# A fused sparse-attention and feed-forward kernel: operands of its matmuls moved to 2 KB multiples, four softmax buffers, and small VectorE work moved to GpSimd and ScalarE

## The chip, the core and the metric

The kernel runs on one core of a Trainium2 chip. The metric is the device time of one execution in microseconds (us), lower is better. Before the change it is 938.36 us, the median of three runs (938.2 to 938.99).

## What is computed

Attention with 8 batches, 8 heads, 576 positions and head size 64, followed by a feed-forward network on the 4608 tokens. Heads 0 to 3 see the 32 newest positions ("local"), heads 4 to 7 see every 32nd position ("strided").

```python
scores = scale * np.matmul(q, k.transpose(0, 1, 3, 2))
mask_local = (rel >= 0) & (rel < stride)
mask_strided = (rel >= 0) & (pos[None, :] % stride == pos[:, None] % stride)
...
attn = np.exp(scores - max); attn = attn / (np.sum(attn, axis=-1, keepdims=True) + 1e-09)
x = np.matmul(attn, v)          # to (4608, 512), all heads side by side
h = x @ w_in                    # (4608, 2048)
g = 0.5 * h * (1.0 + erf(h * inv_sqrt2))
return g @ w_out                # (4608, 512)
```

## The kernel before

The 4608 tokens are nine tiles of 512 tokens (t = 0 to 8), and the hidden size 2048 is 16 slices (f = 0 to 15). A matrix is used as the sum of a rounded part and a small rest ("h" and "l" in the tile names: xlh and xll for the local heads, xsh and xsl for the strided ones, gh and gl for the activations; both parts of a weight slice lie in one slot w_wt), and each product is made of three matmuls.

**The dense steps.** For each t and f, line 672 forms the hidden slice in a PSUM bank: 12 matmuls with a 128x128 stationary block of w_wt and 512 columns of x moving. ScalarE applies Gelu (line 697) and rounds (line 698, gh), VectorE takes the rest (line 700, gl), and line 709 multiplies with the second weight matrix: 12 matmuls with gh or gl stationary and 512 columns of w_wt moving. TensorE's order is written out at the end of the kernel (lines 788 to 798): hidden slice n, then output product n-1. So the Gelu of a slice has one output product and one hidden product of time. In tile 0 the first four slices run in two halves of 256 tokens (HALVES = 4), which makes 96 hidden matmuls of 256 columns; the other 3408 large matmuls move 512 columns.

**Weights.** weights(f) loads a packed slice of 1 MB into a slot and unpacks it: two ScalarE passes (lines 290, 291), a VectorE merge (line 293), a rounding (line 302) and a rest (line 307, VectorE or GpSimd). Slots have one tag "w" with 17 buffers of 8 KB per partition, and the attention of the first rows (tiles 0 and 1) borrows them.

**Local attention of the next tile**, local(t). At step f = 2 TensorE makes the scores of tile t+1 (line 366), at f = 13 the products with v (line 407). Between them, for four groups j: a masked maximum on VectorE (line 426, four instructions, writes a pt tile), four exponentials on ScalarE (line 433), for each pair of groups an addition of 1e-9 and a reciprocal (lines 438, 439), the quotient (line 443, VectorE or GpSimd), a 32x32 transpose (line 447), and eight small DMAs from pt to bt, issued by SyncE (line 396). The pt tiles have two buffers (line 413), so group 2 needs the buffer of group 0 and group 3 that of group 1.

**Strided attention of the next tile**, unit(): GpSimd multiplies (lines 556, 573), VectorE sums (lines 561, 578), and finish() makes the softmax: maximum and subtraction (lines 502, 503), exponential on ScalarE (line 511), sum, addition of 1e-9, reciprocal and product on VectorE (lines 506 to 509). turn() transposes the result (line 518) and split() rounds it on ScalarE (line 324) and takes the rest on VectorE (line 329). opening() does the same for tiles 0 and 1, all batches at once.

**The order.** Every operation is handed to a planner (Plan.add) with the engines that may run it, its cost there, and a due time. Plan.run plays this forward and writes the instructions of each engine in the order that it found; the chip then runs each engine's list in that order. Its costs come from lines 253 to 266 (STEP = 5.43 us for a dense step, T0 = 17 us for the start).

**Output.** Each tile's four PSUM banks are copied to ob tiles (line 716, two buffers) and stored by SyncE (line 728).

In the program's allocation before, the large operands do not start at multiples of 2 KB within a partition: the w slots start 1824 bytes past one, xl 1120, xs 1632, gh and gl 1632.

Of the kernel before, what the change touches and what calls it, by code (L numbers as in the profile page):

```python
# [16 lines left out]
U16 = mybir.dt.uint16  # L17
AF = mybir.ActivationFunctionType
# [3 lines left out]
P = 128  # L22
# [6 lines left out]
UR = 4  # L29
FIRST, VISIT = 2, 13  # L30
HALVES = 4
# [32 lines left out]

class Part:
# [7 lines left out]
class Op:  # L73
    def __init__(self, eng, fn, deps, due, bufs, table, kb, name, rel):
        self.eng, self.fn, self.deps, self.due, self.bufs = eng, fn, deps, due, bufs
        self.table, self.kb, self.name, self.rel = table, kb, name, rel
        self.start = self.end = None


class Plan:  # L80
# [9 lines left out]
    def add(self, eng, fn, deps=(), due=0.0, bufs=(), table=None, kb=0, name="", rel=None):  # L90
        op = Op(eng, fn, [d for d in deps if d is not None], due,
                [b.buf if isinstance(b, Part) else b for b in bufs], table, kb, name,
                due - self.ahead if rel is None else rel)
        for b in op.bufs:
            b.left += 1
        self.ops.append(op)
        return op

    def run(self, busy):
# [8 lines left out]
        nxt, now, state, dma = 0, 0.0, "e", 0.0  # L108
        events = []
# [15 lines left out]
        pe_done = set()  # L125
        h_end = 0.0
        while count < len(self.ops):
            moved = False
            for e in free:
# [3 lines left out]
                for op in waiting[e]:  # L133
# [10 lines left out]
                    if any(room[k] < v for k, v in need.items()):  # L144
                        continue
                    if e == "ACT" and op.table == "e" and state == "g":
                        ready = sum(x.eng[e] for x in waiting[e] if x.table == "e" and at[x] <= now)
                        if (ready < 1.2 and now < at[op] + 5.0) or now - 0.1 < h_end < now + 2.0:
                            continue
# [16 lines left out]
                op.end = now + dur  # L166
                if e == "PE":
# [3 lines left out]
                if op.kb:  # L171
                    dma = max(dma, now + 0.9) + op.kb / 400.0
# [35 lines left out]
def attn_ffn_kernel(ctx: ExitStack, tc: tile.TileContext, qk, vl, vl0, q0, k0, v0, q1, k1, v1, qs, ks, vs, w, out):  # L208
    nc = tc.nc
    NT = qk.shape[0]  # L210
# [26 lines left out]
    def slot(name, dtype=F32):  # L237
        return buf("w", [P, 4 * DM], name, NF + 1, dtype)
# [24 lines left out]
    T0 = 17.0  # L263
    LOSS = 3.4

    def at_step(n):
        return T0 + 2.0 + n * STEP + (n // NF) * LOSS

    def at_pass(n):
        return T0 + n * 2.9 if n < 2 * HALVES else at_step(n - HALVES)  # L270
# [4 lines left out]
    def weights(f):  # L275
        raw, wt = slot(f"raw{f}"), slot(f"wt{f}")
        lead = buf("lead", [P, 2 * DM], f"{f}", 2, F16)
        due = at_pass(f) - 3.0 if f <= HALVES else at_step(f) - 3.0
        views = {}

        def load(e):
# [7 lines left out]
        o0 = plan.add({"SP": 0.5}, load, [lo_of.get(f - 3)], due - 12 if f else 2.3, [raw], kb=1024, name=f"load{f}")  # L289
# [5 lines left out]
            [o2], due - 4, [raw], name=f"or{f}")  # L295
# [8 lines left out]
        o4 = plan.add({"DVE": 0.72, "ACT": 1.16}, hi, [o3], due - 3, [raw, wt], name=f"hi{f}")  # L304
# [4 lines left out]
        o5 = plan.add({"POOL": 2.4} if f > HALVES else {"DVE": 1.25, "POOL": 2.4} if f else {"DVE": 1.25}, lo, [o4], due - 2, [raw, wt], name=f"lo{f}")  # L309
# [4 lines left out]
    def x_bufs(t):  # L314
        local = [buf(f"xl{i}", [P, N2, TT], f"{t}", 1, F32R) for i in "hl"]
        strided = [buf(f"xs{i}", [P, DH, TT], f"{t}", 2, F32R) for i in "hl"]
# [5 lines left out]
    def split(src, dst, bufs, src_bufs, deps, due, n, name, psum_src=True):  # L322
# [7 lines left out]
        o2 = plan.add({"DVE": dve(n)}, low, [o1] + deps, due + 0.3, bufs + src_bufs, name=f"{name}l")  # L330
# [6 lines left out]
    def local(t):  # L337
# [3 lines left out]
        for a, b in ((0, 2), (2, 4)) if t == 0 else ((0, 4),):  # L341
            ld += [plan.add({"SP": 0.5}, lambda e, a=a, b=b: nc.sync.dma_start(
                lq()[:, a * JW:b * JW], qk[t][:, a * JW:b * JW]), [v_ops.get((t - 1, NJ - 1))],
                T + FIRST * STEP - 12 if t else 0.1 + a, [lq], kb=128 * 4 * (b - a) * JW / 1024, name=f"qk{t}")] * (b - a)
# [534 lines left out]
```

## Time and profile before

| | before |
|---|---|
| median of 3 runs | 938.36 us |
| the profiled execution, its own time | 939.23 us |
| its span | 937.5 us |
| mean granted TensorE clock | 0.975 |
| TensorE matmul busy | 870.9 us (93%) |
| VectorE busy | 529.7 us (57%) |
| ScalarE busy | 398.3 us (42%) |
| GpSimd busy | 463.5 us (49%) |

The span is taken inside the execution; 1.7 us of its time lie around it. PE is TensorE's matmuls, PEld its weight loads, DVE VectorE, ACT ScalarE, POOL GpSimd, SP SyncE, and SPq the queue in which SyncE issues DMAs. A busy TensorE is not TensorE at its peak, since matmuls overlap: what counts is the distance from start to start. Idle time of the other engines costs nothing unless TensorE waits for it.

### The profile page before, as it was taken

The page shows a single profiled execution, that of the slowest core. Times are in us where ns is not written, and L with a number is a line of the kernel's source. Part 1 is how long each engine was busy: PE and PEld are TensorE (multiplying, and loading weights), DVE is VectorE, ACT ScalarE, POOL GpSimd, SP SyncE. Part 2 cuts the span into 40 slices and gives each one's busy share as a digit, 9 for nine tenths or more (in the row PEclk, how much of TensorE's full clock was granted, in tenths as well). Part 3 has the DMA queues.
Part 4 walks back from the last instruction along what each step waited for, and adds up shares of the span by engine and source line. Part 5 has one row for each costly group of instructions (what it writes and reads, how often), then busy time and mean ns, then how long its engine had stood idle before and what let it go on. Part 6 is the DMA issues. An engine that isn't in the chain of part 4 may idle for free. (4 is left out here: it accounts for less than half of the span.)

```text
span 937.5 us, 15581 instructions
## 1 busy us (share of the span) xinstructions
PE 870.9 (93%) x6032; PEld 700.3 (75%) x6032; DVE 529.7 (57%) x1110; ACT 398.3 (42%) x808; POOL 463.5 (49%) x325
## 2 busy tenths in 40 slices
PE   2598799989999999899989999899999998999997
PEld 2486587768887888688867878687878886888885
DVE  4879757674667486435856664646676486111111
ACT  4769724643344345433552244433543344122111
POOL 4647576556566576445737754654576483000000
PEclk9999989989999999899998999999999999999999
DMA  9934222210231032002301211012210220001001
GB/s 373 391 135 182 80 69 46 101 34 4 79 117 46 1 124 95 19 3 102 116 12 53 83 49 58 11 58 105 66 58 26 80 73 17 3 1 45 1 1 45
DMA packets 27098, 69.43 MB, mean 74 GB/s; under 512 B 5904, under 2 KB 14096, under 8 KB 24720
## 3 DMA queue, kind: packets, MB, share of 16 engines
q1 hardware_dynamic: 27024, 68.44, 20.8%
q8 instruction: 47, 0.77, 0.3%
q14 instruction: 27, 0.22, 0.1%
HBM read 54.78 MB, written 9.44 MB: 69 GB/s over the span
## 5 line engine op out<-in xcount | busy, mean ns | idle before, releaser
L709 PE MATMUL banks<-w_wt,gh 128*128 128x512 f32 x1152 | 372.4, 405 | 11.3 <-ACT gh L698 11.2
L709 PEld LDWEIGHTS banks<-w_wt,gh 128*128 128x128 f32 x1152 | 220.9, 193 | 66.7 <-ACT gh L698 14.6
L709 PE MATMUL banks<-w_wt,gl 128*128 128x512 f32 x576 | 235.3, 408 | 23.3 <-DVE gl L700 23.3
L697 ACT ACTIVATE banks<-banks 128x512 f32<-128x512 f32 (+1 forms) x148 | 84.6, 571 | 377.2 <-PE banks L672 376.7
L700 DVE TENSOR_TENSOR gl<-banks,gh 128x512 fp32r<-128x512 f32 (+1 forms) x148 | 99.0, 670 | 202.2 <-ACT gh L698 202.0
L672 PE MATMUL banks<-xsh,w_wt 128*128 128x512 f32 (+1 forms) x592 | 165.3, 398 | 7.6 <-DVE w_wt L302 4.5
L672 PE MATMUL banks<-xlh,w_wt 128*128 128x512 f32 (+1 forms) x592 | 159.5, 388 | 0.0
L709 PEld LDWEIGHTS banks<-w_wt,gl 128*128 128x128 f32 x576 | 111.8, 194 | 56.1 <-DVE gl L700 29.5
L672 PEld LDWEIGHTS banks<-xsh,w_wt 128*128 128x128 f32 x592 | 112.3, 194 | 34.1 <-DVE w_wt L302 5.0
L672 PEld LDWEIGHTS banks<-xlh,w_wt 128*128 128x128 f32 x592 | 111.6, 190 | 23.7
L672 PE MATMUL banks<-xsl,w_wt 128*128 128x512 f32 (+1 forms) x296 | 92.4, 391 | 0.2 <-DVE xsl L329 0.2
L672 PE MATMUL banks<-xll,w_wt 128*128 128x512 f32 (+1 forms) x296 | 91.8, 389 | 0.0
L698 ACT CAST gh<-banks 128x512 fp32r<-128x512 f32 (+1 forms) x148 | 85.1, 575 | 4.6
L672 PEld LDWEIGHTS banks<-xsl,w_wt 128*128 128x128 f32 x296 | 56.6, 192 | 13.6 <-DVE xsl L329 0.5
L672 PEld LDWEIGHTS banks<-xll,w_wt 128*128 128x128 f32 x296 | 56.1, 190 | 11.6
L426 DVE CUSTOM_DVE_ANT_0 pt<-banks,mask 128x64 f32<-128x64 f32 x128 | 20.7, 221 | 57.4 <-DMA bt<-pt 53.6
L433 ACT ACTIVATE pt<-pt,lsm 128x64 f32<-128x64 f32 x128 | 42.9, 336 | 21.4 <-DVE lsm L426 16.6
L307 POOL TENSOR_TENSOR w_wt<-w_raw,w_wt 128x1024 fp32r<-128x1024 f32 x13 | 32.7, 2521 | 37.1 <-ACT w_wt L302 21.4
L697 ACT ACT_TABLE_LOAD x39 | 50.0, 1283 | 0.7
L293 DVE SCALAR_TENSOR_TENSOR w_raw<-w_raw 128x1024 uint32<-128x1024 uint32 x16 | 26.6, 1669 | 4.4 <-ACT w_raw L291 4.3
L433 ACT ACT_TABLE_LOAD x18 | 23.1, 1283 | 14.0 <-DMA bt<-pt 10.2
L443 POOL TENSOR_TENSOR pt<-pt,lsm 128x256 f32<-128x256 f32 x13 | 8.6, 662 | 37.7 <-ACT sc_6.3_5051 L511 7.7
(912 smaller groups left out, 1080.7 us busy)
## 6 DMA issues: line engine op xcount, KB each, us to landing
w_raw<-in_w_dram SPq DMA_DIRECT2D x16, 1023.8 KB, 11.3
lq_qk<-in_qk_dram SPq DMA_DIRECT2D x8, 1280.0 KB, 5.7
lq_v<-in_vl_dram SPq DMA_DIRECT2D x8, 1024.0 KB, 5.0
sk<-in_ks_dram SPq DMA_DIRECT2D x8, 576.0 KB, 5.4
sv<-in_vs_dram SPq DMA_DIRECT2D x8, 576.0 KB, 3.6
bt<-pt SPq DMA_DIRECT2D x256, 16.0 KB, 1.8
sq<-in_qs_dram SPq DMA_DIRECT2D x8, 448.0 KB, 4.4
lq_qk<-in_qk_dram SPq DMA_DIRECT2D x2, 640.0 KB, 6.2
```

Of the source, the lines that this page charges most:

```text
L293: o3 = plan.add({"DVE": 1.25}, lambda e: V.scalar_tensor_tensor(views["word"], views["word"], 13, views["other"], ALU.logical_shift_right, ...
L307: (V if e == "DVE" else G).tensor_tensor(views["t"][:, 1, :], views["word"].bitcast(F32), views["t"][:, 0, :].bitcast(F32), ALU.subtract)
L426: V.tensor_tensor_reduce(pt()[:, 256 + h * 64:256 + (h + 1) * 64], sb[j][h % 2]()[:, c + h // 2 * 64:c + (h // 2 + 1) * 64], masks[0 if t ...
L433: A.activation(pv[:, :, h, :], pt()[:, 256 + h * 64:256 + (h + 1) * 64].rearrange("p (c t) -> p c t", c=2), AF.Exp, bias=sm[0]()[:, h:h + ...
L443: (V if e == "DVE" else G).tensor_tensor(pv, pv, sm[2]().unsqueeze(1).unsqueeze(3).to_broadcast([P, 2, HL, QB]), ALU.mult)
L672: nc.tensor.matmul(hp()[:, 0:c1 - c0], w1[f][:, lw, c, :], rx, start=((c, part) == (2, 0)), stop=((c, part) == end))
L697: A.activation(hp()[:, 0:N], hp()[:, 0:N], AF.Gelu)
L698: A.copy(a_()[:, 0:N], hp()[:, 0:N])
L700: o3 = plan.add({"DVE": dve(N)}, lambda e, hp=hp, a_=a_, b_=b_, N=N: V.tensor_tensor(b_()[:, 0:N], hp()[:, 0:N], a_()[:, 0:N].bitcast(F32) ...
L709: nc.tensor.matmul(o, x()[:, sl], w2[f][:, y, :], start=(f == 0 and i == 0), stop=(f == NF - 1 and i == 2))
```

## The change

- A first pool (mats) is padded to a 2 KB multiple and holds the w slots, xl, xs, gh and gl; all of them then start at multiples of 2 KB.
- pt has four buffers instead of two.
- The output goes through quarters of one w slot (Piece), so four copies can be under way instead of two.
- finish() is cut into seven operations. Subtraction and product go to GpSimd (VectorE may take them for tiles 0 and 1), the addition of 1e-9 goes to ScalarE; so does that of local(). The quotient of line 443 is on GpSimd for all tiles but 0, and the rest of the strided x is on GpSimd.
- The planner gets a flag "port": no two flagged operations of VectorE and GpSimd are placed at the same time. Due times are derived from TensorE's order.
- The start: loads are cut into halves in a fixed order (FIRST_DMA), the first tile's keys and values leave out a block that is masked away, opening() works on half of the batches at a time, the masks are made with fewer instructions, and two slices instead of four run in halves (HALVES = 2).

```diff
-HALVES = 4
+HALVES = 2
...
+                    if op.port and e in ("DVE", "POOL") and port > now + 1e-9:
+                        continue
...
+    pad = -(nc.sbuf_base + 31) // 32 * 32 % LINE
+    if pad:
+        ctx.enter_context(tc.tile_pool(name="pad", bufs=1)).tile([P, pad], U8, name="pad")
+    mats = ctx.enter_context(tc.tile_pool(name="mats", bufs=1))
+    pool = ctx.enter_context(tc.tile_pool(name="pool", bufs=1))
     const = ctx.enter_context(tc.tile_pool(name="const", bufs=1))
-    pool = ctx.enter_context(tc.tile_pool(name="pool", bufs=1))
...
-        return buf("w", [P, 4 * DM], name, NF + 1, dtype)
+        return buf("w", [P, 4 * DM], name, NF + 1, dtype, mats)
...
-    T0 = 17.0
+    T0 = 14.0
+    FIRST_DMA = {"q": (0.0, 2.0), "k": (0.1, 2.1), "qk": (0.2, 2.2), "v": (1.5, 5.3), "vl": (1.6, 5.4), "w": (1.0, 4.0, 6.0)}
...
-        o5 = plan.add({"POOL": 2.4} if f > HALVES else {"DVE": 1.25, "POOL": 2.4} if f else {"DVE": 1.25}, lo, [o4], due - 2, [raw, wt], name=f"lo{f}")
+        o5 = plan.add({"POOL": 2.4} if f > HALVES else {"DVE": 1.25}, lo, [o4], due - 2, [raw, wt], name=f"lo{f}", port=True)
...
-            pt = buf("pt", [P, 2 * HL * 2 * QB], f"{t}_{j}", 2)
+            pt = buf("pt", [P, 2 * HL * 2 * QB], f"{t}_{j}", 4)
...
             def third(e, both=both):
-                V.tensor_scalar_add(both()[:, 2 * HL:4 * HL], both()[:, 2 * HL:4 * HL], 1e-9)
+                A.activation(both()[:, 2 * HL:4 * HL], both()[:, 2 * HL:4 * HL], AF.Copy, bias=1e-9)
+
+            def inverse(e, both=both):
                 V.reciprocal(both()[:, 4 * HL:], both()[:, 2 * HL:4 * HL])
...
-                o = plan.add({"POOL": 0.9, "DVE": 0.46}, fourth, [rec], due - 1.5, [pt, both], name=f"quo{t}.{j}")
+                o = plan.add({"POOL": 0.75} if t else {"POOL": 0.75, "DVE": 0.46}, fourth, [rec], due - 1.5, [pt, both], name=f"quo{t}.{j}", port=True)
...
-            V.tensor_tensor(view(), view(), wide(m()[:, 0:n]), ALU.subtract)
-
-        def third(e):
+
+        def second(e):
+            (V if e == "DVE" else G).tensor_tensor(view(), view(), wide(m()[:, 0:n]), ALU.subtract)
...
+        mul = {"POOL": 0.33 + 0.0021 * n * c}
+        if t < 2:
+            mul["DVE"] = 0.25
...
+        return plan.add(mul, seventh, [o], due, [sc, m], name=f"squo{name}", port=True)
...
-            *([xops[t - 1, "s"][0][0]] if t else [])], due, n, f"xs{name}"))
+            *([xops[t - 1, "s"][0][0]] if t else [])], due, n, f"xs{name}", {"POOL": gps(n)} if t > 1 else {"POOL": gps(n), "DVE": dve(n)}))
...
+    obs = slot("ob")
...
-            a_, b_ = buf("gh", [P, TT], f"{n}", 2, F32R), buf("gl", [P, TT], f"{n}", 2, F32R)
+            a_, b_ = [buf(x, [P, TT], f"{n}", 2, F32R, mats) for x in ("gh", "gl")]
...
-            ob = buf("ob", [P, DM], f"{t}.{a}", 2)
+            ob = Piece(plan, obs, a * DM, DM, f"ob{a}")
...
-    for i in range(48):
+    for i in range(47):
```

## Rows read from the trace of the kernel before

**Rows 1.** Page, part 1: busy us (share) and instructions of two engines.
```profile
PE 870.9 (93%) x6032; PEld 700.3 (75%) x6032; DVE 529.7 (57%) x1110; ACT 398.3 (42%) x808; POOL 463.5 (49%) x325
```

**Rows 2.** Waits of TensorE: us in total, times, longest us.
```profile
PE banks L709 <- DVE gl L700: 23.3, 11, 5.3
PE banks L709 <- ACT gh L698: 11.2, 7, 3.6
```

**Rows 3.** Windows: stretch, its us, PE busy (matmuls), granted clock, DMA share, GB/s.
```profile
30.00:64.00 34.00, 28.17 (x143) 0.90 0.65 255
64.00:150.00 86.00, 76.62 (x549) 0.94 0.27 101
150.00:830.00 680.00, 655.78 (x4428) 0.98 0.17 57
```

**Rows 4.** Waits of VectorE: us in total, times, longest us.
```profile
DVE pt L426 <- DMA bt<-pt: 53.6, 16, 5.0
```

**Rows 5.** Timeline, VectorE then TensorE: start, us, engine, line, what [idle before].
```profile
480.14 0.23 DVE L426 CUSTOM_DVE_ANT_0 pt<-banks,mask 128x64 f32<-128x64 f32 x1 [4.17 <-DMA bt<-pt]
...
486.42 0.23 DVE L426 CUSTOM_DVE_ANT_0 pt<-banks,mask 128x64 f32<-128x64 f32 x1 [5.01 <-DMA bt<-pt]
...
490.69 0.73 PE L709 MATMUL banks<-w_wt,gh 128*128 128x512 f32 x2 [2.99 <-ACT gh L698]
493.42 0.79 PE L709 MATMUL banks<-w_wt,gl 128*128 128x512 f32 x1 [2.00 <-DVE gl L700]
```

**Rows 6.** Timeline of TensorE, two steps of tile 4, a half step of tile 0, its first whole step.
```profile
473.62 1.09 PE L672 MATMUL banks<-xsh,w_wt 128*128 128x512 f32 x4
...
475.93 0.62 PE L672 MATMUL banks<-xll,w_wt 128*128 128x512 f32 x2
476.38 0.63 PE L709 MATMUL banks<-w_wt,gh 128*128 128x512 f32 x2
...
479.19 1.10 PE L672 MATMUL banks<-xsh,w_wt 128*128 128x512 f32 x4
...
481.98 0.63 PE L709 MATMUL banks<-w_wt,gh 128*128 128x512 f32 x2
...
51.87 0.63 PE L672 MATMUL banks<-xlh,w_wt 128*128 128x256 f32 x4
52.34 0.40 PE L672 MATMUL banks<-xll,w_wt 128*128 128x256 f32 x2
...
62.94 0.40 PE L672 MATMUL banks<-xsh,w_wt 128*128 128x512 f32 x1
```

**Rows 7.** Timeline of the start: GpSimd, then TensorE.
```profile
9.05 1.26 POOL L609 TENSOR_TENSOR prod_oq0.0.0_243<-w_q,w_k 128x512 f32<-128x512 f32 x1 [2.85 <-DMA w_k<-in_k_dram]
...
20.38 0.31 PE L385 MATMUL banks<-w_pt,w_vl 32*64 32x32 f32 x1 [3.23 <-issue]
...
29.89 1.22 PE L672 MATMUL banks<-xsh,w_wt 128*128 128x256 f32 x4 [3.01 <-ACT xsh L324]
```

**Rows 8.** Whole span, VectorE busy (instructions) of line 503, of 507, of 509.
```profile
0.00:937.50 937.50, 23.84 (x34) 0.98 0.21 74
...
0.00:937.50 937.50, 14.48 (x34) 0.98 0.21 74
...
0.00:937.50 937.50, 12.63 (x34) 0.98 0.21 74
```

**Rows 9.** Groups of instructions: busy us, mean ns | idle before.
```profile
L443 DVE TENSOR_TENSOR pt<-pt,lsm 128x256 f32<-128x256 f32 x19 | 13.2, 705 | 0.1
...
L438 DVE TENSOR_SCALAR lsm<-lsm 128x8 f32<-128x8 f32 x18 | 10.2, 567 | 9.5 <-ACT pt L433 9.5
...
L443 POOL TENSOR_TENSOR pt<-pt,lsm 128x256 f32<-128x256 f32 x13 | 8.6, 662 | 37.7 <-ACT sc_6.3_5051 L511 7.7 <-DVE lsm L439 7.6 <-DVE ssm_4.3_3445 L506 7.4
...
L507 DVE TENSOR_SCALAR ssm_o<-ssm_o 128x16 f32<-128x16 f32 x2 | 2.6, 1310 | 0.1
```

**Rows 10.** Timeline of the end: ScalarE's last copy.
```profile
933.70 0.58 ACT L716 COPY ob_8.3_8000<-banks 128x512 f32<-128x512 f32 x1 [3.16 <-DMA out_dram<-ob_8.1_7990]
```

More of the change, by code (lines that the diff above doesn't have):

```diff
@@ L73, with __init__ @@
 class Op:
-    def __init__(self, eng, fn, deps, due, bufs, table, kb, name, rel):
+    def __init__(self, eng, fn, deps, due, bufs, table, kb, name, rel, port, fixed):
         self.eng, self.fn, self.deps, self.due, self.bufs = eng, fn, deps, due, bufs
         self.table, self.kb, self.name, self.rel = table, kb, name, rel
-        self.start = self.end = None
+        self.start = self.end = self.last = None
+        self.port, self.fixed = port, fixed
 class Plan:
@@ L88, in __init__, with add @@
         self.floating = set()
-    def add(self, eng, fn, deps=(), due=0.0, bufs=(), table=None, kb=0, name="", rel=None):
+    def add(self, eng, fn, deps=(), due=0.0, bufs=(), table=None, kb=0, name="", rel=None, port=False, fixed=False):
         op = Op(eng, fn, [d for d in deps if d is not None], due,
-                [b.buf if isinstance(b, Part) else b for b in bufs], table, kb, name,
-                due - self.ahead if rel is None else rel)
+                [b.buf if isinstance(b, Part) else b for b in bufs] + [
+                    b.buf for b in bufs if isinstance(b, Piece)], table, kb, name,
+                due - self.ahead if rel is None else rel, port, fixed)
         for b in op.bufs:
@@ L108, in run, with latest @@
         nxt, now, state, dma = 0, 0.0, "e", 0.0
+        after = dict(zip(self.pe, self.pe[1:]))
+        late = {}
+        def latest(op):
+            if op not in late:
+                end = op.last if op.last is not None else 1e6
+                for u in users.get(op, ()):
+                    end = min(end, latest(u) - self.LAT)
+                if op in after:
+                    end = min(end, latest(after[op]))
+                late[op] = end - min(op.eng.values()) - (op.kb / 370.0 + 2.0 if op.kb else 0.0)
+            return late[op]
+        import sys
+        sys.setrecursionlimit(100000)
+        for op in reversed(self.ops):
+            op.due = op.due if op.fixed else latest(op)
         events = []
@@ L166, in run @@
                 op.end = now + dur
+                if op.port and e in ("DVE", "POOL"):
+                    port = op.end
                 if e == "PE":
@@ L329, in low @@
             (V if e == "DVE" else G).tensor_tensor(lo, src(), hi.bitcast(F32), ALU.subtract)
-        o2 = plan.add({"DVE": dve(n)}, low, [o1] + deps, due + 0.3, bufs + src_bufs, name=f"{name}l")
+        o2 = plan.add(where or {"DVE": dve(n)}, low, [o1] + deps, due + 0.3, bufs + src_bufs, name=f"{name}l", port=where is not None)
         return o1, o2
@@ new lines, in add @@
+            def add(e, r=r, n=n, p=p):
+                V.tensor_reduce(view()[:, :, r, 0:n],
+                                p()[:, 0:HB * n * D].rearrange("p (b c d) -> p b c d", b=HB, d=D), AX.X, ALU.add)
+            om = times(HB * n * D, mul, [ql, kl, o0], due - 4, [qb, kb_, p], f"oq{name}.{r}", t)
+            sums.append(plan.add({"DVE": dve(HB * n * D)}, add, [om, o0], due - 3.5, [p, sc], name=f"osq{name}.{r}"))
+        o = finish(t, sc, (2 * HB, C), sums, due - 2, name)
+        outs = []
@@ L645, in opening, with mul @@
-        for h in range(2):
-            turn(t, acc, acc, h * 256, TR // 2, outs[h], due + 8 * h * (t == 0), f"o{t}.{h}", off=h * 512)
+            out_ = (lambda r=r: acc()[:, 0:1024].rearrange("p (b r d) -> p b r d", b=B, r=2)[:, bs, r, :])
+            if n == 1:
+                def mul(E, r=r, out_=out_):
+                    E.tensor_tensor(out_(), vv()[:, bs, :, 0], view()[:, :, r, 0:1].to_broadcast([P, HB, D]), ALU.mult)
+                outs.append(times(HB * D, mul, [o, vlo], due - 1, [vb, sc, acc], f"ov{name}.{r}", t))
+                continue
```

221 lines of the change are left out of this document (121 added, 100 removed).

## The prediction

> **What bounds the kernel now.** I read the page first: TensorE's matmuls are busy 93% of the span, VectorE 57%, GpSimd 49% [rows 1]. So TensorE sets the time, and the change can gain in three ways only: a shorter distance between matmuls, fewer waits of TensorE, a shorter start or end. Each has its own view.
>
> The distance I take from starts in TensorE's timeline. A hidden slice of 12 matmuls runs from 473.62 to 476.38, 2.76 us; the output product behind it from 476.38 to 479.19, 2.81; the next hidden slice, with the same x but another weight slot, from 479.19 to 481.98, 2.79 [rows 6]. A dense step is thus about 5.57 us, 0.232 per matmul. The 3408 large matmuls with 512 columns are 142 such steps, 791 us.
>
> The waits: line 709 waits 23.3 us for gl and 11.2 us for gh [rows 2]. After a wait the granted clock falls from 2.4 to 1.2 GHz for a while: its mean is 0.90 from 30 to 64 us, 0.94 from 64 to 150 and 0.98 from 150 to 830 [rows 3]. With matmuls that run at half speed, the missing share is itself lost time: 3.4, 5.2 and 13.6 us, rounding in the last one included.
>
> Where the waits come from stands in VectorE's view: line 426 waits 53.6 us, 16 times, for the DMAs out of pt [rows 4], two waits for each of eight tiles. In tile 4 VectorE stands from 475.97 to 480.14 and from 481.41 to 486.42; the second wait makes exponentials, Gelu and gl late, and TensorE waits 2.99 and 2.00 us at 490.69 and 493.42 [rows 5]. The reader should see that VectorE is idle there, but nothing behind line 426 in its list can pass.
>
> **The change part by part**, against the profiled execution's own 939.2 us (0.9 above the median; its span is 937.5).
>
> *Four pt buffers.* Groups 2 and 3 no longer need the buffers that the DMAs read, so the 16 waits go. Waits of line 709 are 34.5 us and the clock behind them from 64 to 830 us is 18.8 [rows 2, 3]: 53 us. Not all of it hangs on pt, since other VectorE work is held up as well (next part). What is late next is the order of exponentials and Gelus on ScalarE: four exponentials and two table loads in the time between a hidden slice and its use. I take 42 us back (ends: 25, about half, and 53).
>
> *VectorE's small work moved.* Lines 503, 507 and 509 cost VectorE 23.8, 14.5 and 12.6 us for 34 softmaxes [rows 8], lines 443 and 438 another 13.2 and 10.2 [rows 9]: 74 us leave it. A TENSOR_SCALAR of 16 columns took 1.3 us on average [rows 9], far more than its size asks for, so this work was held up by something beside it. GpSimd gets two small products and a rest of x for each of 32 units. The nearest row is 0.66 us for 256 columns [rows 9]; at 0.45 twice and 0.66 once that is 50 us, and 19 quotients add 12.5. It then works about 526 us [rows 1], 66 for each of the eight tiles whose attention runs beside a tile before. It stays hidden, 0 us, as long as a unit's result is ready before its tile begins. But a softmax now passes VectorE, GpSimd, ScalarE, VectorE, ScalarE, VectorE, GpSimd, and VectorE's list stands at the reciprocal until ScalarE has added 1e-9, with gl behind it. No row shows this wait. Bounds: 0 if it falls into VectorE's idle time (43% of the span), and 1.3 us (two ScalarE passes ahead of the addition, estimated at twice and a bit the copy's 0.58 us [rows 10]) at each of some 50 places, 65 us, if all reached TensorE. gl has some 3.5 us to spare in a step, so I take +5, near the lower end.
>
> *2 KB multiples.* The address does matter for the distance: same lines, same x, and 2.76 against 2.79 with another weight slot [rows 6]. The lowest level shown is 0.225 (two matmuls from 475.93 to 476.38). Matmuls of 256 columns stand 0.1175 apart (four in 0.47 from 51.87 [rows 6]), 0.011 above 256 columns at 2.4 GHz; 512 columns with the same extra would take 0.224. I therefore read 0.225 as the undisturbed distance and the rest as a cost of where operands lie. With every operand at a multiple I take 0.226: a step falls from 5.57 to 5.42, times 142 is 21, of which I count 20 us. Ends: 24 us if all reach 0.225; below nothing, 4 us lost, if the hidden matmuls rise to the 2.81 of the output ones (0.03 for each of 142 steps). No operand of before lies at a multiple, so this is the least certain term.
> The Trainium skill (TensorE: Matmul & The Clock Gate, the step list of Part 2) says that TensorE has two independent SBUF read ports and that loading the next weights takes nothing from the running matmul. By that rule placement does nothing and this term is 0.
>
> *The start.* The first dense matmul is at 29.89. GpSimd waits for k until 9.05, and one matmul of the value product comes 3.23 us late with no releaser [rows 7]. The loads ahead of the first products fall from 640 + 512 + 512 KB to 256 + 256 + 512, each product is halved, and the value matmuls fall by a quarter. I estimate the first dense matmul at 21: about 2.5 us from the loads, 3 from products and sums at half size, 3 from the late matmul. Ends: 2 (the late matmul and ScalarE's order remain) and 12. From 29.89 to the end of the halves at 62.94 [rows 6] TensorE needs 22.5 us (96 times 0.1175 and 48 times 0.234) and takes 33, so 10.5 are waits and low clock. Two halved slices instead of four also halve the time in which the second half of x can get ready, from 11 to 5.6 us; that cover is gone, so of these 10.5 I take only 3 back (ends: 5 lost, 8 gained). Together 12 us.
>
> *The output.* At the end, the last copy starts at 933.70 after 3.16 us in which it waits for a store to free its buffer [rows 10]. With four quarters it waits for its bank alone, whose product ends somewhat later than the wait begins, and the stores keep SyncE's order: 2 us (ends: 0 and 3.2). Earlier tiles hide theirs. The slot it takes is one that raw weights no longer need after tile 0: 0. One warm-up matmul less and the masks are covered by the loads: 0.
>
> Sum: 42 - 5 + 20 + 12 + 2 = 71, 939.2 - 71 = 868.
>
> **The rivals.**
> 1. *Placement does nothing*, all else as above: 868 + 20 = 888. For it: a matmul of 256 columns, which here ends within its 2 KB stretch, has the same sort of extra as the best ones of 512, so the extra may belong to the matmul and not to the place. Against it: the two levels above. 22%.
> 2. *The waits come back elsewhere.* ScalarE's order and the new chain keep half of the waits and of the clock: 42 becomes 21, the hops cost 15 and not 5, 868 + 31 = 899. For it: line 438 waits 9.5 us for ScalarE even now [rows 9]. 13%.
> 3. *Placement gives more.* A matmul could fall below the lowest distance of before, if part of the 0.011 is also due to where operands lie; all of it gone is 0.213 per matmul, 5.12 a step, 64 us instead of 20: 824. Against it: no two 512-column starts in these rows stand closer than 0.225 at full clock [rows 6]. 8%. The Trainium skill (TensorE: Matmul & The Clock Gate, Back-to-back issue gap) gives columns/2.4 GHz plus 2.5 ns, an estimated 5.18 a step and 833 in all; the rows of before lie above it.
> 4. *Slower: GpSimd becomes the bound.* It needs about 66 of some 93 us per tile (16 steps of 5.57 and the local attention's small matmuls, an estimate). If each of 4.5 units makes it stand at two new waits, for the exponential and the reciprocal, the last unit's x comes late and TensorE stands at the tile's first slice. It decides where added idle time exceeds the 27 us left, that is 3 us at each of nine waits; at 4.2 us each tile boundary waits 11 us, seven times 11 is 77, 868 + 77 = 945. Against it: the planner knows these costs, and a unit's work can be placed before. 7%.
> 5. *It does not do what it says*: pt is not the cause and padding changes nothing, within 0.2% of 938. Against it: [rows 5]. 2%.
>
> **How the numbers follow.** My forecast has 48%, the rivals 22, 13, 8, 7 and 2. Around 868 the terms' ends reach 847 (all waits gone, start better) and 887. The range reaches up to rival 2 with some margin and down to the forecast's lower end: 845 to 906. That leaves out rivals 3, 4 and 5, 17 in 100, and little of rival 2. Slower by over 0.2%, about what a measurement can tell from no change, is rival 4: 0.07. Within 0.2%: 0.03. Faster: 0.90.
>
> **What would show it.** Right: line 426 has no wait for bt<-pt; waits of line 709 under 10 us in all; granted clock 0.99 or more from 64 us on; 12 hidden matmuls in 2.71 and 12 output ones in 2.72 us in the undisturbed last tile; first dense matmul near 21 us; no 3 us wait of ob. Wrong: the last tile's steps still 5.56 us (rival 1); long waits for gl with VectorE standing at a reciprocal (rival 2); TensorE waiting for xsl or xsh at tile starts with GpSimd busy to the end (rival 4).

## The result and the profile after

The changed kernel takes 882.11 us (median of four runs, 880.88 to 882.36) against 938.28 of the kernel before on the same chip (938.04 to 938.99): a ratio of 0.9398, 95% interval 0.9381 to 0.9414. That is inside the range, 14 us above the forecast of 868. The profiled execution took 880.88 us with a span of 879.0.

Lines have moved: the hidden product is line 741 (672 before), the output product 779 (709), gl 770 (700), the masked maximum 485 (426), the copies to bt 455 (396), the product with v in later tiles 466 (407), the load of weights 325 (283), their rounding 344 (302) and their rest 349 (307).

The page's part 1, which answers to [rows 1]:

```profile
PE 838.0 (95%) x5878; PEld 690.5 (79%) x5878; DVE 443.1 (50%) x946; ACT 410.1 (47%) x868; POOL 503.4 (57%) x433
```

TensorE lost 33 us of busy time, although its large matmuls do the same work: the distance from matmul to matmul and the low clock are part of "busy". VectorE lost 87 us. GpSimd gained 40, not the 62 of the estimate: its small operations took 0.29 and 0.25 us (35 in 10.0 us, 33 in 8.4) where I had put 0.45, and some other work left it.

TensorE's waits for weights, for the copies to bt and those of the output product (us in total, times, longest us), as in [rows 2]:

```profile
PE banks L741 <- ACT w_wt L344: 5.4, 2, 4.6
...
PE banks L741 <- POOL w_wt L349: 4.3, 4, 1.7
PE banks L466 <- DMA bt<-pt: 3.9, 3, 2.2
...
PE banks L779 <- DVE gl L770: 0.8, 1, 0.8
...
PE banks L779 <- ACT gh L768: 0.3, 1, 0.3
```

The 34.5 us for gl and gh are 1.1 now. Hidden slices wait longer for the rounded weights and their rest, 9.7 us in all against 4.5 before, and the product with v waits for the copies to bt (3.9). The windows say where (stretch, its us, PE busy and matmuls, granted clock, DMA share, GB/s), as in [rows 3]:

```profile
64.00:150.00 86.00, 72.72 (x405) 0.92 0.40 154
150.00:830.00 680.00, 680.00 (x4657) 1.00 0.17 56
```

From 150 us on TensorE neither waits nor loses clock: 680 of 680 us at 1.00, against 655.78 at 0.98. But from 64 to 150 us it stands still for 13.3 us where it stood 9.4, and the clock is 0.92 where it was 0.94. That stretch is worse than before.

TensorE's timeline (start, us, line, what [idle before]): the start, as in [rows 7], the bad place in tile 0, a step of tile 4, as in [rows 6], and a hidden slice of the last tile.

```profile
8.63 1.14 PE L413 MATMUL banks<-lq_qk 64*64 64x64 f32 x32 [6.18 <-DMA lq_qk<-in_qk_dram]
...
25.49 1.20 PE L741 MATMUL banks<-xsh,w_wt 128*128 128x256 f32 x4 [2.44 <-ACT w_pt L492]
...
118.98 0.42 PE L466 MATMUL banks<-bt,lq_v 64*64 64x32 f32 x12 [2.20 <-DMA bt<-pt]
...
134.43 0.80 PE L741 MATMUL banks<-xsh,w_wt 128*128 128x512 f32 x1 [4.63 <-ACT w_wt L344]
136.91 1.65 PE L741 MATMUL banks<-xsh,w_wt 128*128 128x512 f32 x3 [1.69 <-POOL w_wt L349]
...
468.69 1.07 PE L741 MATMUL banks<-xsh,w_wt 128*128 128x512 f32 x4
...
471.41 0.62 PE L779 MATMUL banks<-w_wt,gh 128*128 128x512 f32 x2
...
474.13 1.07 PE L741 MATMUL banks<-xsh,w_wt 128*128 128x512 f32 x4
...
865.44 1.07 PE L741 MATMUL banks<-xsh,w_wt 128*128 128x512 f32 x4
...
868.16 0.62 PE L779 MATMUL banks<-w_wt,gh 128*128 128x512 f32 x2
```

The start-to-start times show the new distance: 468.69 to 471.41 and 471.41 to 474.13, both 2.72, and the hidden slice of the last tile too (865.44 to 868.16). That is 0.2267 us per matmul for either product; [rows 6] had 2.76 to 2.81 for the twelve. The first dense matmul comes at 25.49 (29.89 before, 21 forecast).

SyncE's DMA issues between 98 and 122 us show where the last load of weights in tile 0 now stands (start, time from first to last issue, line, what, how many):

```profile
98.66 21.56 SPq L455 DMA_DIRECT2D bt<-pt  x32
120.33 0.52 SPq L325 DMA_DIRECT2D w_raw<-in_w_dram  x1
```

32 copies out of the four pt buffers are issued in a row, 0.67 us each, and the last load of weights stands behind them. The kernel before issued 16 copies, the load, and the other 16 copies:

```profile
98.74 10.11 SPq L396 DMA_DIRECT2D bt<-pt  x16
108.95 0.53 SPq L283 DMA_DIRECT2D w_raw<-in_w_dram  x1
119.49 10.01 SPq L396 DMA_DIRECT2D bt<-pt  x16
```

So the load comes 11.4 us later now. Its place is not the only reason why these weights are late. It lands 5.0 us after its issue, at about 125.3, but ScalarE begins to unpack it at 128.19. In its list that work stands behind the Gelu of a hidden slice, and this slice came late because the product with v ahead of it waited for the last copies:

```profile
127.09 0.58 ACT L767 ACTIVATE banks<-banks 128x512 f32<-128x512 f32 x1 [11.95 <-PE banks L741]
...
128.19 1.12 ACT L332 CAST lead<-w_raw 128x1024 f16<-128x1024 bf16 x1
```

**The ledger.** The last 3340 large matmuls are the same work in both kernels, so I compare when the matmul starts that has a given number still to come, itself counted, over both products' lines in the trace. One thing shifts between the marks: TensorE makes the scores of tile 1 with 3300 to come before and with 3348 to come after, since two slices fewer run in halves. They push the next large matmul back by 1.5 us (a distance of 1.73 us instead of 0.23), so at the mark 3340 the changed kernel leads by 8.3 us in equal work, not 6.8.

| large matmuls still to come | before | after | gained so far |
|---|---|---|---|
| 3340 | 68.98 | 62.23 | 6.8 |
| 3200 | 108.60 | 98.04 | 10.6 |
| 3100 | 143.26 | 140.05 | 3.2 |
| 1 | 930.92 | 873.38 | 57.5 |

Of the 54.3 us gained behind the 3100th, about 15.6 are the distance (the mean of all undisturbed 512-column distances fell from 232.0 to 227.0 ns; 3100 times 5.03 ns). The rest, 38.7, is waits and low clock: the windows from 150 to 830 give much the same, 24.2 us of idle time and 2% of 680 us, 37.8 in all. What follows the last matmul's start fell from 6.6 to 5.6 us; the last copies wait for their bank alone, no longer for a store.

### The profile page after: what moved, and what is told of

Same layout as the page of the kernel before. It is cut to its first block, busy times and chain, and to the rows that moved or that the text cites. A ratio compares the mean times of both kernels' runs of the same rounds, so it can differ in the third digit from the quotient of the medians.

```text
span 879.0 us, 15285 instructions
## 1 busy us (share of the span) xinstructions
PE 838.0 (95%) x5878; PEld 690.5 (79%) x5878; DVE 443.1 (50%) x946; ACT 410.1 (47%) x868; POOL 503.4 (57%) x433
## 4 chain that ended last, share of the span: by engine, by line
PE 84%; ACT 6%; DMA 4%; DVE 2%; SPq 2%; issue 1%; POOL 0%; ACTq 0%
PE banks L741 41%; PE banks L779 40%; DMA w_raw<-in_w_dram 3%; PE banks L466 2%; DVE w_raw L335 2%; SPq L455 2%; ACT lead L332 1%; PE banks L425 1%; ACT w_raw L333 1%; DMA w_kv<-in_v_dram 1%; ACT pt L492 1%; ACT w_wt L344 1%; ACT L492 1%; ACT L767 1%; ACT banks L767 1%
## 5 line engine op out<-in xcount | busy, mean ns | idle before, releaser
L779 PE MATMUL banks<-w_wt,gh 128*128 128x512 f32 x1152 | 355.0, 389 | 0.3 <-ACT gh L768 0.3
L779 PEld LDWEIGHTS banks<-w_wt,gh 128*128 128x128 f32 x1152 | 216.2, 188 | 45.3 <-ACT gh L768 0.7
L779 PE MATMUL banks<-w_wt,gl 128*128 128x512 f32 x576 | 224.4, 390 | 0.8 <-DVE gl L770 0.8
L741 PE MATMUL banks<-xsh,w_wt 128*128 128x512 f32 (+1 forms) x584 | 162.5, 398 | 12.3 <-ACT w_wt L344 5.4
L741 PEld LDWEIGHTS banks<-xsh,w_wt 128*128 128x128 f32 x584 | 109.2, 191 | 38.0 <-POOL w_wt L349 6.8
L779 PEld LDWEIGHTS banks<-w_wt,gl 128*128 128x128 f32 x576 | 108.1, 188 | 24.0 <-DVE gl L770 1.7
L741 PEld LDWEIGHTS banks<-xsl,w_wt 128*128 128x128 f32 x292 | 55.8, 192 | 11.6
L741 PEld LDWEIGHTS banks<-xll,w_wt 128*128 128x128 f32 x292 | 55.4, 190 | 11.6 <-DVE xll L371 0.2
L349 POOL TENSOR_TENSOR w_wt<-w_raw,w_wt 128x1024 fp32r<-128x1024 f32 x13 | 32.1, 2472 | 21.1 <-ACT w_wt L344 11.6
L504 POOL TENSOR_TENSOR pt<-pt,lsm 128x256 f32<-128x256 f32 x32 | 21.0, 676 | 26.1 <-DVE lsm L500 12.2
L335 DVE SCALAR_TENSOR_TENSOR w_raw<-w_raw 128x1024 uint32<-128x1024 uint32 x16 | 31.1, 1952 | 4.1 <-ACT w_raw L333 3.8
L466 PEld LDWEIGHTS banks<-bt,lq_v 64*64 64x64 f32 x1024 | 20.2, 134 | 7.1 <-issue 3.9
```

The source lines that it names most:

```text
L335: o3 = plan.add({"DVE": 1.25}, lambda e: V.scalar_tensor_tensor(views["word"], views["word"], 13, views["other"], ALU.logical_shift_right, ...
L349: (V if e == "DVE" else G).tensor_tensor(views["t"][:, 1, :], views["word"].bitcast(F32), views["t"][:, 0, :].bitcast(F32), ALU.subtract)
L466: nc.tensor.matmul(xb[b]()[half(i), c:c + QB], vv[half(b), a, 2 * r + i, :], bv[half(b), a, 2 * r + i, :], start=True, stop=True, tile_pos ...
L504: (V if e == "DVE" else G).tensor_tensor(pv, pv, sm[2]().unsqueeze(1).unsqueeze(3).to_broadcast([P, 2, HL, QB]), ALU.mult)
L741: nc.tensor.matmul(hp()[:, 0:c1 - c0], w1[f][:, lw, c, :], rx, start=((c, part) == (2, 0)), stop=((c, part) == end))
L779: nc.tensor.matmul(o, x()[:, sl], w2[f][:, y, :], start=(f == 0 and i == 0), stop=(f == NF - 1 and i == 2))
```

## The experiments

Before's median on the chip of a group stands with it.

### Where operands lie (kernel before: 937.18; for the last of the three 935.79)

**All large operands together at 1824 bytes past a 2 KB multiple.**

```diff
-    pad = -(nc.sbuf_base + 31) // 32 * 32 % LINE
+    pad = -(nc.sbuf_base + 31) // 32 * 32 % LINE - 224
```

> The changed kernel with the large operands all moved together from a multiple of 2 KB to 1824 bytes past one. Theory A (the place against 2 KB multiples matters): the 12 matmuls of an output product take 2.78 to 2.81 us again instead of 2.72, those of a hidden slice 2.75 to 2.80, and the time rises by 14 to 20 us, to 896 to 902. Theory B (what matters is that all operands have the same offset, since reads of the moving and of the stationary operand then don't meet): 2.72 stays, 882. Theory C (placement never mattered, the order of instructions did): 2.72 stays, 882; the next run tells B from C.

Measured: 881.56 us (two runs, ratio 0.9411, 0.9363 to 0.9459), the time of the changed kernel. TensorE's timeline, tile 4:

```profile
470.53 1.07 PE L741 MATMUL banks<-xsh,w_wt 128*128 128x512 f32 x4
...
473.25 0.62 PE L779 MATMUL banks<-w_wt,gh 128*128 128x512 f32 x2
...
475.97 1.07 PE L741 MATMUL banks<-xsh,w_wt 128*128 128x512 f32 x4
```

Both products still take 2.72 us, although every operand of 2 KB now crosses a 2 KB boundary. The multiple itself does nothing.

**Only the weights at 2 KB multiples**, x, gh and gl 672 bytes past one.

```diff
-        local = [buf(f"xl{i}", [P, N2, TT], f"{t}", 1, F32R, mats) for i in "hl"]
+        local = [buf(f"xl{i}", [P, N2, TT], f"{t}", 1, F32R, xmat) for i in "hl"]
...
-            a_, b_ = [buf(x, [P, TT], f"{n}", 2, F32R, mats) for x in ("gh", "gl")]
+            a_, b_ = [buf(x, [P, TT], f"{n}", 2, F32R, xmat) for x in ("gh", "gl")]
```

> The changed kernel with the weight slots still at 2 KB multiples, but x, gh and gl about 0.7 KB past one. In a hidden slice x moves and the weights are stationary; in an output product the weights move and gh, gl are stationary. If the moving operand's place matters: hidden slices slow (2.75 to 2.80 us for 12), output products at 2.72, about 890. If the stationary operand's place matters: hidden slices 2.72, output products slow, about 890. If only equal offsets matter (theory B): both slow, about 899. If placement never mattered (theory C): both 2.72, 882.

Measured: 899.89 us (one run), 18 more than the changed kernel. TensorE's timeline:

```profile
470.75 1.08 PE L742 MATMUL banks<-xsh,w_wt 128*128 128x512 f32 x4
...
473.54 0.63 PE L780 MATMUL banks<-w_wt,gh 128*128 128x512 f32 x2
...
476.35 1.10 PE L742 MATMUL banks<-xsh,w_wt 128*128 128x512 f32 x4
```

2.79 and 2.81 us: both products are slow, and each has one operand at a multiple, the hidden one the stationary blocks, the output one the moving columns. What counts is where the two operands of a matmul lie relative to each other.

**Small differences**: weights at 1824 bytes, xl 64, xs 128, gh and gl 256 bytes further.

```diff
-    pad = -(nc.sbuf_base + 31) // 32 * 32 % LINE
+    pad = -(nc.sbuf_base + 31) // 32 * 32 % LINE - 224
...
+    mats_xl = shifted("mats_xl", 64)
+    mats_xs = shifted("mats_xs", 64)
+    mats_g = shifted("mats_g", 128)
...
```

> The changed kernel with weight slots at one offset, xl 64 bytes further, xs 128, gh and gl 256 (all counted modulo 2 KB). It asks how equal the offsets must be for 2.72 us per 12 matmuls. If a difference of any size costs: hidden slices 2.76 to 2.82 and output products 2.76 to 2.82, about 895 to 900. If a multiple of 64 bytes is enough: 2.72 everywhere, 882. If a multiple of 256 is needed: output products 2.72, hidden slices slow, in both the part with xs and the part with xl. If a multiple of 512 is needed (the slices of a stationary operand lie 512 bytes apart): all slow.

Measured: 895.12 us (one run), about 15 more. TensorE's timeline:

```profile
470.29 1.09 PE L747 MATMUL banks<-xsh,w_wt 128*128 128x512 f32 x4
...
471.68 1.09 PE L747 MATMUL banks<-xlh,w_wt 128*128 128x512 f32 x4
...
473.07 0.63 PE L785 MATMUL banks<-w_wt,gh 128*128 128x512 f32 x2
...
475.84 1.09 PE L747 MATMUL banks<-xsh,w_wt 128*128 128x512 f32 x4
```

The six matmuls with xs (128 bytes off) take 1.39 us, the six with xl (64 off) 1.39, the twelve with gh and gl (256 off) 2.77; undisturbed they are 1.36, 1.36 and 2.72. So each of the three differences costs. Differences of a multiple of 512 bytes cost nothing: the stationary blocks are 512 bytes wide, so in the changed kernel they lie 0, 512, 1024 or 1536 bytes past the moving operand's place, and all run at 0.2267. In the kernel before all large operands were 192 bytes, modulo 512, before the place of the weights (1120 and 1632 against 1824). Why equal places are faster is open, and other widths or types were not tried.

### Who took the waits away (kernel before: 935.79, or 937.18 for the kernel with VectorE's small work and the first one with two buffers)

**Four pt buffers alone, in the kernel before** (the output in quarters of a weight slot, which makes the room).

```diff
-            pt = buf("pt", [P, 2 * HL * 2 * QB], f"{t}_{j}", 2)
+            pt = buf("pt", [P, 2 * HL * 2 * QB], f"{t}_{j}", 4)
...
-            ob = buf("ob", [P, DM], f"{t}.{a}", 2)
+            ob = Piece(plan, obs, a * DM, DM, f"ob{a}")
```

> The kernel before with four pt buffers, and with the output in quarters of a weight slot, which makes the room for them. Theory A (the buffers alone take the waits away, and in the changed kernel something else also does): line 426 no longer waits for bt<-pt, line 709 waits under 10 us, 895 to 912. Theory B (the order that the planner finds is what counts): VectorE's wait moves to something else that is issued in the same order, line 709 still waits 20 us or more, 920 to 940.

Measured: 895.4 us (one run), 40.4 less, of which 1.5 lies behind the last matmul's start (5.1 us in place of 6.6). VectorE has no wait for bt<-pt left. TensorE's waits for gl, and the windows:

```profile
PE banks L723 <- DVE gl L714: 8.1, 9, 1.7
```

```profile
64.00:150.00 86.00, 82.59 (x588) 1.00 0.32 113
150.00:800.00 650.00, 645.77 (x4443) 1.00 0.17 58
```

Without the 16 stalls of VectorE the waits for gl fall from 23.3 to 8.1 us, and the clock is full from 64 us on. The mechanism of the prediction and its size (42) hold.

**The planner's price of the copies alone, in the kernel before.** The changed kernel also raises the cost that the planner books for eight copies to bt (a line that the cut diff ahead leaves out).

```diff
-                o = plan.add({"SP": 3.6}, send, [o], due, [pt, bt], kb=128,
+                o = plan.add({"SP": 4.4}, send, [o], due, [pt, bt], kb=1400,
```

> The kernel before, with nothing but the planner's cost of the eight small DMAs out of pt changed as in the change (4.4 us of SyncE's queue and 1400 KB instead of 3.6 us and 128 KB). Theory B1 (the planner put the maxima of groups 2 and 3 too early because it held those DMAs for cheap): waits of line 426 fall to 25 us or less and those of line 709 to 15 or less, 900 to 920. Rival (the two buffers themselves, or the due times): waits as before, 930 to 945.

Measured: 901.55 us (one run), 34 less, with two buffers. VectorE's wait for the copies, and a window:

```profile
DVE pt L426 <- DMA bt<-pt: 22.0, 14, 3.2
```

```profile
150.00:800.00 650.00, 648.76 (x4457) 1.00 0.18 59
```

VectorE still waits 22 us, but TensorE hardly notices: from 150 us on it is as good as without waits. The planner, told that the copies take long, orders VectorE's list otherwise; which moves did it I did not follow.

**Two pt buffers in the changed kernel**, first alone:

```diff
-            pt = buf("pt", [P, 2 * HL * 2 * QB], f"{t}_{j}", 4)
+            pt = buf("pt", [P, 2 * HL * 2 * QB], f"{t}_{j}", 2)
```

> The changed kernel with two pt buffers instead of four. Theory: VectorE stands at its maximum (line 485) for the DMAs out of pt again, 16 times and some 45 to 55 us in all, line 779 waits 15 to 35 us, the granted clock falls in most tiles, and the time rises by 25 to 40 us to 907 to 922. Rival (VectorE's relief from small work removed the waits, the buffers did not): VectorE still waits there, but gl has enough time to spare, and the time stays within 885 to 892.

Measured: 878.47 us (two runs, ratio 0.9378, 0.9321 to 0.9435): not slower. VectorE's wait for the copies, a window of TensorE, SyncE's queue near the end of tile 0 and TensorE's wait for the copies:

```profile
DVE pt L485 <- DMA bt<-pt: 11.9, 7, 3.5
```

```profile
150.00:800.00 650.00, 650.00 (x4526) 1.00 0.18 60
```

```profile
107.91 0.53 SPq L325 DMA_DIRECT2D w_raw<-in_w_dram  x1
118.16 11.20 SPq L455 DMA_DIRECT2D bt<-pt  x16
```

```profile
PE banks L466 <- DMA bt<-pt: 7.2, 8, 2.1
```

So in the changed kernel the buffers are not needed. Nor do they cost tile 0 anything: with two of them the last load goes out 12.4 us earlier than with four and no slice waits for the last weights, but the product with v waits 7.2 us for the last 16 copies, and the matmul with 3100 to come starts at 139.92, as with four (140.05). Then with the due times as written, too, in place of those derived from TensorE's order:

```diff
-            op.due = op.due if op.fixed else latest(op)
+            latest(op)
```

> The changed kernel with two pt buffers and with due times as they are written in the program, not derived from TensorE's order. Theory B2 (with due times from TensorE's order gl and Gelu go ahead of the maxima that would wait, which is why two buffers cost nothing there): TensorE waits 15 us or more for gl and gh beyond 150 us, 895 to 930. Rival B1 (the cost of the DMAs alone): no such waits, within 5 us of 880.

Measured: 877.34 us (one run), with 650 of 650 us at full clock from 150 on, so the due times are not what replaces the buffers; the price of the copies, which is left, does so in the kernel before. (Two buffers, the old price and all else of the change were not tried together, and the change's other planner lines were not run by themselves.)

**VectorE's small work back on VectorE** from tile 1 or 2 on (only the addition of 1e-9 stays on ScalarE).

```diff
-                o = plan.add({"POOL": 0.75} if t else {"POOL": 0.75, "DVE": 0.46}, fourth, [rec], due - 1.5, [pt, both], name=f"quo{t}.{j}", port=True)
+                o = plan.add({"DVE": 0.46} if t else {"POOL": 0.75, "DVE": 0.46}, fourth, [rec], due - 1.5, [pt, both], name=f"quo{t}.{j}", port=True)
...
-        mul = {"POOL": 0.33 + 0.0021 * n * c}
-        if t < 2:
-            mul["DVE"] = 0.25
+        mul = {"DVE": 0.25} if t > 1 else {"POOL": 0.33 + 0.0021 * n * c, "DVE": 0.25}
...
```

> The changed kernel with the softmaxes' subtraction and product, the quotient and the rest of the strided x on VectorE for tiles 1 or 2 to 8, as before the change; the additions of 1e-9 stay on ScalarE. Theory (moving them was worth something, since VectorE was held up by GpSimd's work beside it): waits for gl come back in some tiles, time 890 to 905. Rival (VectorE has enough idle time, and only pt mattered): no waits beyond 150 us, time within 4 us of 882, or some 3 us less because the chain of engines is shorter.

Measured: 880.86 us (two runs, ratio 0.9403, 0.9345 to 0.9462): no difference. The page's part 1:

```profile
PE 837.4 (95%) x5878; PEld 690.3 (79%) x5878; DVE 516.3 (59%) x1073; ACT 416.3 (47%) x873; POOL 450.1 (51%) x305
```

73 us are back on VectorE and TensorE notices nothing, in either direction.

### Buffers and common place together, in the kernel before (937.39)

The output is in quarters here too, as with the buffers alone.

```diff
+    mats = ctx.enter_context(tc.tile_pool(name="mats", bufs=1))
...
-        return buf("w", [P, 4 * DM], name, NF + 1, dtype)
+        return buf("w", [P, 4 * DM], name, NF + 1, dtype, mats)
...
-            pt = buf("pt", [P, 2 * HL * 2 * QB], f"{t}_{j}", 2)
+            pt = buf("pt", [P, 2 * HL * 2 * QB], f"{t}_{j}", 4)
```

> The kernel before with two parts of the change only: four pt buffers (with the output staged in quarters of a weight slot, which makes room for them) and a common offset of weights, x, gh and gl, modulo 2 KB. If these two carry the gain and do not hang together, the waits give about 40 us (as with the buffers alone, 895) and the distance of 0.2267 us per 512-column matmul in place of 0.232 gives about 17: 878 to 881 us, within 4 us of the changed kernel, with no wait of TensorE over 2 us beyond 150 us. Rival: the small work on GpSimd or the halved start carry part of it after all; then this kernel keeps waits beyond 150 us or a distance above 0.228 and stays above 886.

Measured: 880.27 us (four runs, ratio 0.9389, 0.9364 to 0.9415), 15 us less than with the buffers alone (17 by the ratios to each chip's own before) and level with the changed kernel. TensorE's waits and windows:

```profile
PE banks L726 <- DVE gl L717: 9.5, 9, 2.0
```

```profile
64.00:150.00 86.00, 81.72 (x591) 1.00 0.33 113
150.00:800.00 650.00, 645.43 (x4494) 1.00 0.18 59
```

The time is as expected, the path is not quite: waits for gl remain. By the ledger the matmul with 3340 to come starts at 68.51 here and at 62.23 in the changed kernel; with 3100 to come it is 133.36 against 140.05, and the last at 873.76 against 873.38. So the rest of the change (start, small work, due times, price of copies) gains 7.8 us at the start (the 1.5 us of scores counted), loses 14.5 in the rest of tile 0 and gains 7.1 afterwards: nothing in the sum.

### The last weights of tile 0 (kernel before: 937.39; for the last of the three 937.65)

**The copies of groups 2 and 3 wait for the last load**, and the product with v of tile 1 is placed two steps later.

```diff
-                o = plan.add({"SP": 4.4}, send, [o], due, [pt, bt], kb=1400, name=f"send{t}.{j}")
+                o = plan.add({"SP": 4.4}, send, [o] + ([load_of[NF - 1]] if t == 1 and j > 1 else []), due, [pt, bt], kb=1400, name=f"send{t}.{j}")
...
-        if t < NT - 1 and f == VISIT:
+        if t < NT - 1 and f == (VISIT if t else NF - 1):
```

> The changed kernel, where the copies to bt of groups 2 and 3 of tile 1 may only be issued once the load of weights 15 has been, and the value product of tile 1 is placed a step later. Theory: the last weights come late because 32 copies stand ahead of their load in SyncE's queue from 98.7 to 120.2 us; issued before them, the load takes away the waits of the last two hidden slices (5.4 and 4.3 us at lines 344 and 349) and the half clock behind them: 8 to 14 us less, 868 to 874. Rival: the load is bound by bandwidth or the rounding on ScalarE and GpSimd by their own order; then the wait stays or comes back at another place and the time is 879 to 884.

Measured: 870.66 us (four runs, ratio 0.9289, 0.9270 to 0.9308), 11 less than the changed kernel (10 by the ratios, whose intervals lie apart) and 67 less than before: the fastest version here, with that of the next experiment. SyncE's queue and TensorE's waits:

```profile
98.72 10.12 SPq L455 DMA_DIRECT2D bt<-pt  x16
111.98 0.33 SPq L325 DMA_DIRECT2D w_raw<-in_w_dram  x1
115.30 10.32 SPq L455 DMA_DIRECT2D bt<-pt  x16
```

```profile
PE banks L741 <- POOL w_wt L349: 6.0, 5, 1.9
...
PE banks L741 <- ACT w_wt L344: 0.7, 1, 0.7
```

The load is issued 8.4 us earlier, and the wait of 4.6 us is gone; so is the product's wait for the copies. With 3340 large matmuls to come this kernel stands at 62.25, as the changed one does. With 3100 to come it is 127.05 against 140.05, but here the product with v, 2.5 us, is still ahead. With 3080 to come both have it behind them, at 134.26 and 144.61: 10.4 us are won in between, and nothing afterwards. The edit moves the load and the product together, so this run does not tell what each is worth.

**The load of q and k for the scores (lq_qk, the "score weights" of the expectation) first in the queue.**

```diff
-    FIRST_DMA = {"q": (0.0, 2.0), "k": (0.1, 2.1), "qk": (0.2, 2.2), "v": (1.5, 5.3), "vl": (1.6, 5.4), "w": (1.0, 4.0, 6.0)}
+    FIRST_DMA = {"q": (0.1, 2.1), "k": (0.2, 2.2), "qk": (0.0, 2.0), "v": (1.5, 5.3), "vl": (1.6, 5.4), "w": (1.0, 4.0, 6.0)}
```

> The changed kernel with the load of the score weights first in the queue, as in the kernel before, ahead of q and k. Theory: the first scores wait until 8.6 us for it because it is third in the queue and shares the bandwidth with the loads ahead of and behind it; put first, the wait at the first score product ends 1 to 3 us earlier and the first dense matmul comes 2 to 3 us before 25.5: 878 to 880. Rival: the loads q, k and qk end together wherever they stand in the queue; then the first dense matmul stays within 0.5 us of 25.5 and the time at 880 to 882.

Measured: 871.94 us (four runs, ratio 0.9300, 0.9281 to 0.9320): 10 less, far more than either expectation, and for another reason. TensorE's timeline, then SyncE's queue:

```profile
5.02 1.13 PE L413 MATMUL banks<-lq_qk 64*64 64x64 f32 x32 [2.58 <-DMA lq_qk<-in_qk_dram]
...
23.05 1.19 PE L741 MATMUL banks<-xsh,w_wt 128*128 128x256 f32 x4 [1.69 <-DVE xll L371]
...
33.34 0.80 PE L741 MATMUL banks<-xsh,w_wt 128*128 128x256 f32 x2 [4.57 <-DVE w_wt L349]
```

```profile
72.43 5.04 SPq L455 DMA_DIRECT2D bt<-pt  x8
...
111.61 0.34 SPq L325 DMA_DIRECT2D w_raw<-in_w_dram  x1
```

The first scores come 3.6 us earlier and the first dense matmul 2.4, as the theory said. But TensorE then waits 4.57 us for rounded weights, and with 3340 matmuls to come it stands at 62.40, where it was 62.23: the lead is given back. The 10 us come from tile 0's end, since the planner, with another start, places half of the copies at 72 to 83 us already, and the last load goes out at 111.61 in place of 120.33. The product with v stays in its place here and waits for no copy; with 3080 to come this kernel stands at 134.89, 9.7 us ahead of the changed one.

**Both edits together.**

> Both edits together: qk first in the queue, and the copies of groups 2 and 3 of tile 1 behind the load of weights 15. Theory: the two took away the same wait, that of the last hidden slices of tile 0 for the last weights (their load is issued at 112.0 and 111.6 us in place of 120.3), and qk's place has no gain of its own, since the same dense matmul (the 3340th from the end) starts at 62.2 to 62.4 us in the changed kernel and in both: 868 to 873, the same as either alone. Rival: the edits have separate causes and add: 858 to 864.

Measured: 876.17 us (four runs, ratio 0.9343, 0.9321 to 0.9365): they don't add, but it is 4 to 6 us slower than either alone, which neither theory said. With 3080 to come it stands at 140.10. The last load is issued at 112.96. The matmul with 3340 to come starts at 63.75, 1.4 us later than in either, and from 100 us on three waits for weights are left (3.60 us at 105.14, 3.52 at 109.16, 1.87 at 129.48), the first two as in the kernel with qk first (3.59 and 3.53). What makes the earlier weights late in this order of loads was not tried.

## Why the prediction was right, and where it was off

**Four pt buffers, 42 us, less 5 for the hops: right in size, half right in attribution.** In the kernel before the buffers alone give 40.4. In the changed kernel waits and clock behind the first 140 us gave 38.7. But the buffers are not what the gain depends on there: the planner's new price of the copies takes most of the same waits away (34 us alone), and the changed kernel with two buffers is no slower. I read the diff's planner lines and priced none of them.

**2 KB multiples, 20 us: right in size, wrong in name.** Measured: 15 to 17 (buffers with and without a common place), 18 (weights alone aligned), 17 by the mean distance. The step is 2 times 2.72, 5.44 against the 5.42 forecast. The reason given, that every operand should lie at a multiple, is refuted: at 1824 bytes the time is the same, and alignment of the weights alone is as slow as before. It is the equal place, modulo 512 bytes, of the two operands of a matmul. The reading behind the term was wrong too: 2.76 against 2.79 is not the weight slot, since all slots lay 1824 bytes past a multiple, and the slot of f = 1 gave 2.76 us in three of the tiles 1 to 8 and 2.80 in five. So that the term came out was partly luck. Rival 1 is refuted, and so is rival 3: no distance below 0.2267 became the rule. The Trainium skill (TensorE: Matmul & The Clock Gate, step list of Part 2) has two independent read ports and weight loads that take nothing from the running matmul. By that the place of one operand against the other should not matter; in these 512-column matmuls it did, and moving one by 64 to 256 bytes took the distance from 0.2267 to 0.231 us. Whether the ports are the reason is not shown.

**VectorE's small work moved, -5 us: nothing.** The run with it back on VectorE is level: neither the 73 us nor the new hops reach TensorE, which fits VectorE's idle time (43% before). The lower bound (0) was the value to take. Rivals 2 and 4 needed waits for gl or x beyond 150 us, and there are none.

**The start, 12 us: this is the step that failed.** Of the 8.9 us by which the first dense matmul should come earlier, 4.4 came. I counted the smaller loads but not the order of the queue, in which the load of q and k for the scores had gone from first to third: the first scores came at 8.63 us, and the run with that load first has them at 5.02 (but gives its lead back to the first weights). The lead with 3340 matmuls to come is 8.3 us in equal work, not 12.

**The rest of tile 0: the order of SyncE's queue was not priced.** It gives 5.0 us back where I expected a further 13 (1.4 of distance, and 11.6 of the 42, since 14.6 of the 53 us of waits and clock lay between 64 and 150 [rows 3]). The prediction did not ask in which order the copies to bt and the last load share SyncE's queue. 32 copies now go out in one piece ahead of the load; first the product with v waits for the last copies and then a hidden slice for the last weights, both with the low clock behind them (0.67 granted from 120 to 140 us). An order that avoids both waits is worth 10 us (870.66 us; a kernel other than the one forecast). The buffers are not the cause: with two of them the product waits longer and the weights do not, and tile 0 ends at the same time.

**The output, 2 us: 1.0.**

In all, tile 0 gave 3.2 us where the steps say about 25, the rest 55.3 where they say 46; the difference, 12.5, is that between 868 and the profiled 880.9. So the total came as near as 14 us partly by luck: some 22 us too little in tile 0 and 9 too much behind it. Of the signs named ahead, no wait of the maximum for bt<-pt, 1.1 us of waits of the output product, 2.72 us for each product and no wait for a store held; the clock from 64 us on (0.92 to 150) and the first dense matmul did not.

## What to carry to other kernels

For matmuls like these (stationary blocks of 512 bytes per partition, 512 columns moving), give the two operands the same place modulo 512 bytes in their partitions before paying for any larger alignment, and check it by the start-to-start times of one undisturbed step. When a change lets producers run ahead, look at what their DMAs now push back in the queue, and at who waits for the last of them: here 32 copies went out ahead of a load, and another order of copies, load and the product that needs the copies was 10 us faster. A ledger by matmuls still to come compares kernels only between marks behind which the same other work lies. Two remedies for one wait don't add; run each alone before crediting either.

## What the runs showed of the hardware that was not expected

A 512-column matmul takes 0.2267 us when both operands lie at the same place modulo 512 bytes and 0.231 to 0.234 when they differ by 64 to 256 bytes modulo 512, whether or not a moving row of 2 KB crosses a 2 KB boundary. In the kernel with lq_qk first, a load's place in the queue, first instead of third, moved its first users from 8.63 to 5.02 us, while the DMA engines were 94 to 95% busy over the first 30 us in both.
